# One product for G and b, pairs of full products early in TensorE's queue, and a new order of the first 911 steps

## The chip, the core and the metric

The kernel runs on one core of one Trainium2 chip. The core has five engines with queues of their own, each strictly in its program's order: TensorE (PE, with its weight loads PEld), VectorE (DVE), ScalarE (ACT), GpSimd (POOL) and SyncE (SP), which here issues all DMAs. The metric is the device time of one execution in microseconds; lower is better.

## The reference

Three parts follow one another: a gated linear attention with a running maximum, and two hidden layers.

```python
for t in range(S):                                # B=4, H=8, S=768, D=40
    m_new = maximum(f[t] + m, i[t])
    C = exp(f[t] + m - m_new) * C + exp(i[t] - m_new) * outer(v[t], k[t])
    n = exp(f[t] + m - m_new) * n + exp(i[t] - m_new) * k[t]
    y[t] = sigmoid(o[t]) * (C @ q[t]) / maximum(abs(n @ q[t]), 1)
x = y as (3072, 320)
h = x @ w_in;  x = (h * clip(h + 3, 0, 6) / 6) @ w_out       # 320 -> 2048 -> 320
h = x @ w_in2; out = square(maximum(h, 0)) @ w_out2          # 320 -> 2048 -> 320
```

## The kernel before

**Attention** goes by units: one batch b and one chunk c of 64 positions, all 8 heads; 48 units, in the order (b, c) = (0,0) (1,0) (0,1) (1,1) (2,0) (3,0) (2,1) (3,1), then by chunk. gate_m, gate_g, gate_G and gate_b are scans and sums over the gates on VectorE, once for chunks 0 to 3 and once for the rest. They give G, a running sum of log forget gates, and b, the log input gate less the maximum and G. A unit's weights are exp(G[query] + b[key] + causal mask). For units 0 to 15, w_pe makes the exponent on TensorE in PSUM (Wp) and w_e takes exp on ScalarE. For units 16 and on, at_gload, w_add and w_mask make it from a DMA and GpSimd. at_S is q times k (Sp, fp32, 16 small products), at_P multiplies it by the weights (VectorE), x_k scales keys, at_Y makes the output and the new state (Yp, 32 small products of 41 columns), at_C copies the state on for the batch's next unit, and at_n1, at_n2, at_n3 divide by max(|n q|, 1) and multiply by the output gate's sigmoid (o_load, o_sig), into X.

**w_pe before**: a product of the mask; then the row b and, per head, G. Rows 0 to 63 of the tile pre hold for each batch a table R of which row belongs to which head (head_rows), and gb holds b as high and low part. For chunks 0 and 1 a unit has eight products of 64 columns that pick G's row (sel, L383) and one of 512 columns for b (L386). For chunks 2 and 3 G is read back through a DMA (at_G, at_R) into four more rows of pre, so one product of 68 rows does it.

**Hidden layers** go by slots: mm_A (L650, hps), one group of 128 hidden units for 512 columns (for slots 0 to 15: 256), eight products; act1, act1b, act2, act2b on ScalarE and VectorE; mm_B (L691, acc), for each 128 tokens three products of 320 columns. Slot s is (layer, block of tokens, group). t_pe, t_hi, t_lo transpose X into high and low parts (xs) for mm_A. Weights arrive as 64-bit floats and are made into high and low parts by w_load (DMA), w_exp (ScalarE), w_b1, w_b2 (VectorE), w_hi (ScalarE) and w_lo (GpSimd, or VectorE with @v); w_load:0,i is group i//2, in-weights for even i.

**Order.** Everything is issued in one list: first FIRST, a list of steps written out (name:unit or name:slot,part; a suffix @v, @a or @g puts the step on VectorE, ScalarE or GpSimd), then the rest in an order that the function moe makes. Each engine takes its own instructions from that list in order and waits where data or buffers are not ready. FIRST reaches to about slot 39 of 200. Buffers that matter: qkt has 3, kI 3, Z 2 for each batch, Sp, tp and Wp of units 8 and on share one PSUM buffer ("s"). Gp (G as high and low part) shares its buffer with the last out-weights, w_load:0,15, and pre shares one of two with xs.

**warm** before: warm:4 issues four fp32 products of 512 columns at the start, on the identity.

Of the kernel before, what the change touches and what calls it, by code (L numbers as in the profile page):

```python
# [37 lines left out]
at_n2:0 at_S:2 x_k:2 w_e:3 at_P:1,0 w_exp:0,2 w_pe:4 w_lo:0,0@v at_load:5 w_pe:5 w_b1:0,2 w_e:4  # L38
at_n3:0 w_load:0,4 w_exp:0,1 at_Y:1 at_P:2,0 w_load:0,10 w_e:5 w_b1:0,1 at_Y:2 at_C:1 at_n1:1
at_S:3 x_k:3 at_n1:2 at_C:2 at_n2:2 w_pe:6 w_load:0,6 at_n2:1 at_n3:2@g at_P:3,0 w_e:6 at_n3:1  # L40
at_Y:3 w_b2:0,2 t_pe:0,0,0 at_C:3 w_pe:7 at_n1:3 t_hi:0,0,0 at_load:6 w_hi:0,2 at_n2:3 at_n3:3
w_e:7 t_lo:0,0,0 w_lo:0,2 w_exp:0,4 t_pe:0,0,1 t_hi:0,0,1 t_lo:0,0,1 w_b1:0,4 at_R mm_A:0
w_exp:0,10 w_load:0,5 w_b2:0,4 mm_A:1 act1:0 w_b2:0,1 w_hi:0,4 at_S:4 act1b:0 x_k:4 act1:1
at_load:7 act2:0 act1b:1 w_lo:0,4 w_hi:0,1 act2b:0 at_P:4,0 mm_A:2 w_exp:0,6 load_gates:1 act2:1
at_S:5 w_lo:0,1 act1:2 act2b:1 w_load:0,3 act1b:2 at_Y:4 at_P:5,0 act2:2 x_k:5 mm_A:3 at_C:4
act2b:2 at_load:8 w_b1:0,6 w_exp:0,5 mm_A:4 w_b2:0,6 act1:3 at_S:6 act1:4 w_load:0,8 w_b1:0,5
w_hi:0,6 mm_B:0,0 w_b2:0,5 mm_B:0,1 mm_B:1,1 act1b:3 x_k:6 w_hi:0,5 mm_B:1,0 at_P:6,0 act2:3
w_lo:0,5 act2b:3 at_load:9 w_pe:8 w_exp:0,3 at_n1:4 mm_A:5 at_n2:4 w_e:8 w_lo:0,6 w_load:0,7
act1b:4 at_Y:5 act1:5 act2:4 act1b:5 w_pe:9 at_C:5 act2b:4 w_e:9 at_n3:4@g at_n1:5 mm_A:6 at_n2:5
o_load:1 at_S:7 w_b1:0,3 act1:6 w_b2:0,3 w_exp:0,8 at_Y:6 act1b:6 x_k:7 w_hi:0,3 at_P:7,0  # L50
w_load:0,14 at_C:6 w_lo:0,3 at_n1:6 at_S:8 x_k:8@a at_n2:6 at_Y:7 at_P:8,0 at_n3:6@g mm_B:2,1
at_n1:7 mm_B:3,1 at_n3:5 w_exp:0,7 t_pe:0,0,2 w_load:0,9 mm_B:4,1 at_n2:7 at_C:7 mm_B:2,0
t_hi:0,0,2@v at_n3:7@g mm_B:3,0 act2:5 t_lo:0,0,2 at_Y:8 act2:6 act2b:5 o_sig:1 t_pe:0,0,3 act2b:6
mm_B:4,0 w_load:0,12 w_b1:0,7 mm_B:5,1 mm_B:5,0 w_b2:0,7 mm_A:7 w_b1:0,8 t_hi:0,0,3 w_b2:0,8 act1:7
w_hi:0,7 at_load:10 t_lo:0,0,3 at_C:8 w_lo:0,7 act1b:7 w_hi:0,8 mm_A:8 at_n1:8 w_load:0,13 act2:7
at_S:9 act1:8 x_k:9@v w_exp:0,9 act1b:8 w_lo:0,8 mm_B:6,0 at_P:9,0 mm_B:6,1 act2:8 at_n2:8@a
act2b:8 w_pe:10 at_load:11 act2b:7 mm_B:8,3 gate_m:1 mm_A:9 at_load:12 mm_A:10 w_exp:0,12 gate_g:1
w_load:0,11 mm_B:7,1 act1:9 mm_B:7,0 act1:10 act1b:9 gate_G:1 at_Y:9 w_e:10 mm_B:8,2 act1b:10
act2:9 at_S:10 x_k:10 act2b:9 w_exp:0,13 at_load:13 w_b1:0,10 mm_A:11 act2:10 at_C:9 act2b:10
mm_B:9,3 w_exp:0,14 w_b2:0,10 mm_A:12 o_load:2 act1:11 at_P:10,0 w_hi:0,10 mm_B:10,3 act1b:11  # L60
w_pe:11 w_load:0,15 act1:12 at_n3:8 mm_B:9,2 act2:11 act1b:12 w_lo:0,10 mm_B:10,2 w_e:11 act2b:11
act2:12 at_n1:9 mm_A:13 w_exp:0,11 act2b:12 w_b1:0,9 o_load:3 mm_A:14 act1:13 w_b1:0,12 mm_B:11,3
act1b:13 act1:14 at_S:11 x_k:11 at_n2:9 act2:13 act1b:14 o_sig:2 mm_B:11,2 act2b:13 at_load:14
mm_B:12,2 w_b2:0,9 mm_A:15 w_b2:0,12 mm_B:13,2 mm_B:12,3 act1:15 at_P:11,0 mm_B:13,3 act2:14
act1b:15 w_pe:12 w_hi:0,12 act2b:14 at_Y:10 gate_b:1 act2:15 w_e:12 mm_A:16 gate_bT:1 o_load:5
act2b:15 at_C:10 mm_B:14,2 o_load:4 at_n1:10 act1:16 at_S:12 x_k:12 w_lo:0,12@v w_hi:0,9 mm_B:15,2
mm_B:14,3 at_n2:10@a at_P:12,0 w_lo:0,9 mm_B:15,3 at_load:15 act1b:16 w_pe:13 mm_A:17 w_b1:0,11
w_e:13 w_b2:0,11 act2:16 at_n3:9 at_Y:11 w_hi:0,11 act2b:16 at_n3:10@g w_pe:14 act1:17 at_n1:11
mm_B:16,0 w_e:14 w_lo:0,11 mm_B:16,2 act1b:17 at_C:11 mm_B:16,1 at_n2:11 act2:17 at_S:13 o_sig:3
act2b:17 x_k:13 mm_A:18 at_P:13,0 at_n3:11@g at_load:16 w_b1:0,13 mm_B:17,2 act1:18 mm_A:19  # L70
w_b2:0,13 w_exp:0,15 act1b:18 w_hi:0,13 w_b1:0,15 mm_B:17,0 act2:18 w_b2:0,15 at_Y:12 act1:19
act2b:18 w_lo:0,13 w_pe:15 at_gload:16 at_gload:17 at_C:12 mm_B:16,3 at_n1:12 w_e:15 mm_A:20
act1b:19 w_add:17 at_n2:12@a w_b1:0,14 at_S:14 w_b2:0,14 mm_B:17,3 mm_B:18,3 at_P:14,0 w_mask:17
# [810 lines left out]
```

## Time and profile before

| | us |
|---|---|
| median of 3 runs (lowest, highest) | 844.32 (844.25, 846.9) |
| the profiled execution | 845.29 |
| its span, first to last instruction | 843.4 |
| TensorE busy, share of the span | 829.6, 98% |
| VectorE, ScalarE, GpSimd busy | 524.8, 433.4, 205.6 |
| mean granted TensorE clock | 0.972 |

The granted clock is the share of 2.4 GHz that TensorE was given; 0.50 is 1.2 GHz. Busy TensorE time includes products at either clock. A wait names the instruction that ended it.

### The profile page before, as it was taken

Reading aid. Unit: us, or ns where it says so; the run is one execution under the profiler, and the core shown is the slowest. Engines: PE = TensorE matmul, PEld = TensorE weight load, DVE = VectorE, ACT = ScalarE, POOL = GpSimd, SP = SyncE. Lnnn points to the kernel's source line nnn. Section 1 sums busy time; section 2 is a strip of 40 time slices with the busy share of each in tenths; the row PEclk is TensorE's granted clock in tenths of the full one; section 3 lists DMA queues with packets and bytes.
Section 4 is the critical chain, followed back from the end, with each engine's and each line's share of the span. In section 5 each row is a group of like instructions: output and inputs, shape, how many; then the busy total and the mean of one; then the engine's idle time right before and its main releaser. Section 6 shows DMA issues by size and latency. Waiting matters only on the chain.

```text
span 843.4 us, 19370 instructions
## 1 busy us (share of the span) xinstructions
PE 829.6 (98%) x8040; PEld 735.3 (87%) x8040; DVE 524.8 (62%) x947; ACT 433.4 (51%) x805; POOL 205.6 (24%) x191
## 2 busy tenths in 40 slices
...
GB/s 220 179 216 186 184 69 96 114 110 88 78 93 108 102 91 118 86 108 21 2 52 194 205 99 1 1 33 1 30 3 1 32 1 2 32 1 1 31 1 32
DMA packets 28843, 63.67 MB, mean 75 GB/s; under 512 B 4912, under 2 KB 17264, under 8 KB 28752
## 3 DMA queue, kind: packets, MB, share of 16 engines
...
q14 instruction: 24, 0.20, 0.1%
HBM read 58.39 MB, written 4.03 MB: 74 GB/s over the span
## 4 chain that ended last, share of the span: by engine, by line
PE 94%; ACT 2%; issue 2%; DVE 2%; POOL 1%; ACTq 0%; POOLq 0%; DVEq 0%
PE hps L650 41%; PE acc L691 39%; PE Yp L504 4%; PE tp L626 2%; PE Sp L470 2%; PE Sp L462 1%; PE Wp L383 1%; PE Sp L464 1%; PE Wp L386 1%; PE Wp L376 1%; PE Sp L477 0%; ACT qs L446 0%; ACT X L698 0%; ACT g L659 0%; DVE qs L448 0%
## 5 line engine op out<-in xcount | busy, mean ns | idle before, releaser
L650 PE MATMUL hps<-xs,wi 128*128 128x512 f32 (+1 forms) x1600 | 390.4, 387 | 1.2 <-ACT xs L630 1.1
L691 PE MATMUL acc<-wo,gh 128*128 128x320 f32 x1536 | 350.0, 315 | 0.2 <-POOL wo L611 0.2
L650 PEld LDWEIGHTS hps<-xs,wi 128*128 128x128 f32 x1600 | 288.2, 191 | 50.9 <-ACT xs L630 1.5
L691 PEld LDWEIGHTS acc<-wo,gh 128*128 128x128 f32 x1536 | 259.8, 189 | 10.5 <-POOL wo L611 0.4
L691 PE MATMUL acc<-wo,gl 128*128 128x320 f32 x768 | 238.0, 310 | 0.0
L681 DVE TENSOR_TENSOR gl<-g,gh 128x512 fp32r<-128x512 f32 x176 | 127.5, 726 | 65.5 <-ACT gh L676 64.7
L671 DVE TENSOR_TENSOR g<-g 128x512 f32<-128x512 f32 x96 | 66.4, 692 | 127.6 <-ACT g L661 127.1
L691 PEld LDWEIGHTS acc<-wo,gl 128*128 128x128 f32 x768 | 144.9, 189 | 0.0
L676 ACT CAST gh<-g 128x512 fp32r<-128x512 f32 x172 | 106.5, 619 | 66.8 <-DVE g L671 53.4
L659 ACT ACTIVATE g<-hps,three 128x512 f32<-128x512 f32 (+1 forms) x104 | 68.1, 656 | 132.0 <-PE hps L650 128.7
L661 ACT ACTIVATE g<-hps 128x512 f32<-128x512 f32 x96 | 57.4, 598 | 151.4 <-PE hps L650 149.5
L668 DVE SCALAR_TENSOR_TENSOR g<-g,hps 128x512 f32<-128x512 f32 x80 | 54.7, 684 | 52.9 <-ACT g L659 52.8
L426 POOL TENSOR_TENSOR Xm<-qkt,W 40x512 f32<-40x512 f32 x27 | 35.8, 1324 | 92.4 <-ACT W L416 74.6
L611 POOL TENSOR_TENSOR wi<-wt,wi 128x768 fp32r<-128x768 f32 x13 | 24.9, 1916 | 108.5 <-ACT wi L606 100.0
L504 PEld LDWEIGHTS Yp<-Z,Xm 104*32 104x32 f32 (+1 forms) x3072 | 35.7, 111 | 16.5 <-issue 14.4
L393 POOL TENSOR_TENSOR W<-W,bT 104x512 f32<-104x512 f32 x32 | 43.5, 1358 | 20.5 <-DVE rd L517 9.0
L448 DVE SCALAR_TENSOR_TENSOR qs<-qs,less,qkt 120x512 fp32r<-120x512 f32 x52 | 40.2, 813 | 9.7 <-ACT qs L446 9.4
L504 PE MATMUL Yp<-Z,Xm 104*32 104x41 f32 (+1 forms) x3072 | 41.8, 210 | 2.8 <-issue 2.8
L437 POOL TENSOR_TENSOR Xm<-kI,W 104x320 f32<-104x320 f32 x37 | 33.7, 911 | 36.5 <-ACT W L406 21.6
L611 POOL TENSOR_TENSOR wo<-wt,wo 128x640 fp32r<-128x640 f32 x16 | 26.6, 1661 | 37.0 <-ACT wo L606 28.1
L446 ACT CAST qs<-qkt 120x1024 fp32r<-120x1024 f32 x26 | 27.2, 1048 | 7.2 <-PE acc L691 3.5
L543 DVE TENSOR_TENSOR X<-X,yt 64x320 f32<-64x320 f32 x34 | 25.3, 743 | 0.9
(110 smaller groups left out, 688.8 us busy)
## 6 DMA issues: line engine op xcount, KB each, us to landing
...
```

The costliest lines, as they stand in the source:

```text
L393: on("w_add", "g", u).tensor_tensor(out=W, in0=W, in1=bT[:, c - NC1, b * H:(b + 1) * H].unsqueeze(2).to_broadcast([KX, H, L]), op=ALU.add)
L448: nc.vector.scalar_tensor_tensor(out=y[0:KS, i], in0=y[0:KS, i].bitcast(F32), scalar=less[0:KS, i:i + 1], in1=x[0:KS, i], op0=ALU.mult, op ...
L504: nc.tensor.matmul(out=Yp[o:e, h, :], lhsT=Xm[:, h, o:e], rhs=Z[b][c % 2][:, h, :], start=True, stop=True)
L611: on("w_lo", "g", ph, i).tensor_tensor(out=w[:, 1], in0=f, in1=w[:, 0].bitcast(F32), op=ALU.subtract)
L650: nc.tensor.matmul(out=h, lhsT=w[:, hl, kk, o:o + P], rhs=t[:, xk, i0 * P:i1 * P], start=(i == 0), stop=(i == len(TERMS) - 1))
L659: nc.scalar.activation(out=g, in_=T["h", s], func=ACTF.Relu, bias=three)
L661: nc.scalar.activation(out=g, in_=T["h", s], func=ACTF.Relu)
L668: nc.vector.scalar_tensor_tensor(out=g, in0=r, scalar=6.0, in1=T["h", s], op0=ALU.min, op1=ALU.mult)
L671: nc.vector.tensor_tensor(out=g, in0=r, in1=r, op=ALU.mult)
L676: copy("act2", s)(out=gh, in_=g)
L681: nc.vector.tensor_tensor(out=gl, in0=g, in1=gh.bitcast(F32), op=ALU.subtract)
L691: nc.tensor.matmul(out=acc[i], lhsT=g[:, n], rhs=w[:, hl, m % MG, :], start=(m == 0 and q == 0), stop=(m == NM - 1 and q == 2))
```

## The change

Chunks 0 to 3 now take one product of 128 rows. A new step, at_rg, writes into rows 64 to 127 of pre the table R times G of the unit's chunk; gb has ones there, so the product sums b and G. The eight products per head, sel, const_s, at_G, at_R and the DRAM buffer Gd1 go. at_load becomes at_qk, at_kn and at_va. at_n1 takes the reciprocal first, clears its sign bit, and the minimum with 1 moves into at_n2 (or stays in at_n1 where ScalarE does at_n2). warm:i issues two bf16 products of 128 rows and 512 columns; 13 such steps stand in the first part of FIRST. FIRST is new.

```diff
 FIRST = """
-const_z:1 const_i warm:4 load_gates:0 const_o head_rows:3 at_load:0 const_m const_l const_g const_z:3
-head_rows:1 o_load:0 const_z:0 const_z:2 at_load:1 const_k:1 const_k:0 gate_m:0 w_load:0,0 gate_g:0
-at_S:0 gate_G:0 const_s at_G:0 gate_b:0 at_load:2 o_sig:0 gate_bT:0@v head_rows:0@v w_load:0,2
-at_S:1 const_k:2 w_pe:0 head_rows:2@g w_pe:1 w_e:0 at_G:1 w_load:0,1 w_exp:0,0 w_pe:2 at_P:0,0
-x_k:0 w_e:1 w_b1:0,0 at_Y:0 at_load:3 w_e:2 w_b2:0,0 w_pe:3 at_C:0 at_n1:0 x_k:1 w_hi:0,0 at_load:4
...
+const_g load_gates:0 const_z:0 const_z:2 const_i const_z:3 warm:1 const_m const_l head_rows:1
+const_z:1 const_o warm:8 at_kn:0 head_rows:3 at_kn:1 const_k:2 warm:13 const_k:0 at_qk:0 const_k:1
+head_rows:2 at_qk:1 warm:16 gate_m:0 at_qk:2 at_va:0 warm:18 gate_g:0 head_rows:0 at_va:1 at_S:0
+gate_G:0 at_va:2 at_qk:3 gate_b:0 at_S:1 at_rg:0@v gate_bT:0 at_kn:2 at_va:3 w_load:0,0 w_pe:0
+at_rg:1@v o_load:0 w_load:0,1 w_pe:1 w_e:0 at_rg:2 w_load:0,4 warm:22 warm:23 w_e:1 at_qk:4 x_k:0@v
+at_P:1,0 w_pe:2 at_rg:3 w_exp:0,0 warm:25 at_P:0,0 x_k:1 w_e:2 warm:33 at_Y:0 at_kn:3 w_b1:0,0
+w_load:0,2 at_Y:1 w_b2:0,0 o_sig:0 w_load:0,7 w_pe:3 at_S:2 at_rg:4@v at_n1:0 x_k:2 w_pe:4 at_n2:0
+at_S:3 at_rg:5 at_C:0@v at_qk:5 w_exp:0,1 at_n1:1 warm:35 at_n2:1 w_hi:0,0 at_n3:0@g warm:36
+at_P:2,0 warm:37 w_e:3 at_va:4 w_lo:0,0@v at_Y:2 at_va:5 warm:38 at_n3:1 at_va:6 w_exp:0,4 at_P:3,0
+w_pe:5 at_va:7 x_k:3@v at_va:8 at_S:4 at_C:1 at_rg:6@v at_C:2 w_e:4 at_Y:3 at_va:9 at_n1:2
+w_exp:0,2 at_n2:2 w_pe:6 at_rg:7 at_n1:3 at_n3:2@g w_e:5 at_n2:3 w_e:6 w_pe:7 at_P:4,0 at_kn:4
+at_rg:8 w_exp:0,7 at_kn:5 t_pe:0,0,0 w_e:7 w_load:0,5 at_n3:3 at_C:3 w_load:0,3 w_b1:0,2 t_hi:0,0,0
+at_qk:6 w_b2:0,2 at_qk:7 at_kn:6 t_lo:0,0,0 w_hi:0,2 x_k:4 at_kn:7 t_pe:0,0,1 w_b1:0,1 at_Y:4
+t_hi:0,0,1 w_b2:0,1 at_va:10 t_lo:0,0,1 w_lo:0,2 w_hi:0,1 at_n1:4 w_exp:0,5 mm_A:0 w_load:0,10
...
+act1b:9 act2:8 at_S:8 act2b:8 x_k:8@a act2:9@v mm_A:10 w_b1:0,9 gate_G:1 mm_B:8,3 o_sig:2 mm_B:8,2
...
+at_n2:13 at_S:14 at_n3:13 w_exp:0,15 x_k:14 mm_B:17,3 act1:21 at_P:14,0 at_gload:18 mm_B:18,3
...
-    NC0 = 2
-    KW = 2 * BH + 2 * (NC1 - NC0)
     pre = xs_p.tile([P, 5, TB], F32R, tag="xs", name="pre")
-    R = [pre[0:KW, b] for b in range(B)]
-    gb = pre[0:KW, B, 0:NC1 * KX].rearrange("p (c k) -> p c k", k=KX)
-    sel = pre[0:2 * BH, B, NC1 * KX:NC1 * KX + BH]
+    R = [pre[0:2 * BH, b] for b in range(B)]
+    RG = [pre[2 * BH:P, b] for b in range(B)]
+    gb = pre[:, B, 0:NC1 * KX].rearrange("p (c k) -> p c k", k=KX)
...
         nc.vector.memset(gb[0:2 * BH].bitcast(F32), 0.0)
-
-        k = slice(2 * BH, KW)
-        shape = [KW - 2 * BH, NC1 - NC0, KX]
-        nc.vector.memset(gb[k, 0:NC0].bitcast(F32), 0.0)
-        nc.vector.tensor_tensor(
-            out=gb[k, NC0:], in0=ident[k, 2 * BH:KW:2].unsqueeze(2).to_broadcast(shape),
-            in1=ident[k, 2 * BH + 1:KW:2].unsqueeze(2).to_broadcast(shape), op=ALU.add)
+        nc.vector.memset(gb[2 * BH:P].bitcast(F32), 1.0)
...
+    def at_rg(u):
+        b, c = units[u]
+        on("at_rg", "g", u).tensor_tensor(
+            out=RG[b].rearrange("p (h l) -> p h l", l=L),
+            in0=R[b].rearrange("p (h l) -> p h l", l=L).bitcast(F32),
+            in1=Gp[:, c * L:(c + 1) * L].unsqueeze(1).to_broadcast([2 * BH, H, L]).bitcast(F32),
+            op=ALU.mult)
...
-        k = KW
-        if c < NC0:
-            k = 2 * BH
-            for h in range(H):
-                j = b * H + h
-                nc.tensor.matmul(
-                    out=Wp[:, h * L:(h + 1) * L], lhsT=sel[:, j:j + 1].to_broadcast([k, KX]),
-                    rhs=Gp[:, c * L:(c + 1) * L], start=False, stop=False)
-        nc.tensor.matmul(out=Wp, lhsT=gb[0:k, c], rhs=R[b][0:k], start=False, stop=True)
+        nc.tensor.matmul(out=Wp, lhsT=gb[:, c], rhs=pre[:, b], start=False, stop=True)
...
+        nc.vector.reciprocal(out=rd, in_=Yp[0:L, :, D:DV])
+        bits = rd.bitcast(I32)
         nc.vector.tensor_scalar(
-            out=rd, in0=Yp[0:L, :, D:DV], scalar1=-1.0, scalar2=1.0, op0=ALU.mult, op1=ALU.max)
-        nc.vector.tensor_tensor(out=rd, in0=Yp[0:L, :, D:DV], in1=rd, op=ALU.max)
-        nc.vector.reciprocal(out=rd, in_=rd)
+            out=bits, in0=bits, scalar1=2 ** 31 - 1, scalar2=None, op0=ALU.bitwise_and)
+        if ENG.get(("at_n2", u)) == "a":
+            nc.vector.tensor_scalar(out=rd, in0=rd, scalar1=1.0, scalar2=None, op0=ALU.min)
...
-            nc.vector.tensor_tensor(
-                out=yt[p0:p0 + L], in0=Yp[0:L, :, 0:D], in1=rd.to_broadcast([L, H, D]),
-                op=ALU.mult)
+            nc.vector.scalar_tensor_tensor(
+                out=yt[p0:p0 + L], in0=rd.to_broadcast([L, H, D]), scalar=1.0,
+                in1=Yp[0:L, :, 0:D], op0=ALU.min, op1=ALU.mult)
...
-    def warm(n):
+    def warm(i):
+        one = ident.bitcast(BF16)
         t = ps_acc.tile([P, TB], F32, tag="acc1", name="warm")
-        for _ in range(n):
+        for _ in range(2):
             nc.tensor.matmul(
-                out=t, lhsT=ident, rhs=ident.unsqueeze(1).to_broadcast([P, TB // P, P]),
+                out=t, lhsT=one[:, 0:P], rhs=one.unsqueeze(1).to_broadcast([P, TB // (2 * P), 2 * P]),
                 start=True, stop=True)
```

## Rows read from the trace of the kernel before

**Rows 1.** Windows by stage: length, busy PE, PEld, DVE, ACT, POOL, clock, DMA share, GB/s.
```profile
0.00:11.40 11.40, 8.67 (x81) 5.02 (x81) 9.51 (x28) 7.54 (x9) 4.26 (x18) 1.00 0.71 205
11.40:39.60 28.20, 27.15 (x397) 22.22 (x397) 13.18 (x33) 12.28 (x22) 6.89 (x7) 0.51 0.64 215
39.60:52.40 12.80, 12.79 (x160) 11.84 (x161) 8.48 (x16) 6.46 (x12) 4.81 (x4) 0.50 0.34 108
52.40:67.20 14.80, 12.02 (x283) 10.21 (x284) 9.11 (x26) 9.65 (x22) 6.62 (x6) 0.96 0.91 323
67.20:73.20 6.00, 6.00 (x89) 5.54 (x83) 3.42 (x10) 2.04 (x6) 1.53 (x2) 0.50 0.82 210
73.20:90.00 16.80, 15.78 (x274) 14.02 (x274) 14.58 (x28) 15.42 (x32) 4.96 (x5) 1.00 0.28 82
90.00:200.00 110.00, 110.00 (x1651) 94.15 (x1650) 90.72 (x186) 79.05 (x194) 52.52 (x49) 1.00 0.44 121
200.00:385.00 185.00, 182.38 (x2316) 161.03 (x2314) 143.59 (x268) 103.64 (x173) 88.39 (x79) 1.00 0.35 93
```

**Rows 2.** Windows of 0.5 us where the granted clock turns, same columns.
```profile
11.50:12.00 0.50, 0.50 (x3) 0.39 (x3) 0.22 (x1) 0.16 (x2) 0.00 (x0) 0.72 0.80 173
...
52.50:53.00 0.50, 0.50 (x5) 0.50 (x5) 0.47 (x2) 0.21 (x1) 0.00 (x0) 0.82 0.83 174
```

**Rows 3.** The chain that ended last, in order of time: start, length, what.
```profile
10.94 0.43 DVE pre L277
...
12.35 1.26 PE Wp L383 x8
...
13.62 0.55 PE Wp L386
...
14.16 0.43 PE Wp L376
...
20.06 0.26 PE Sp L462
...
21.95 0.59 PE Wp L376
...
39.20 0.36 ACT xs L630
...
39.61 4.03 PE hps L650 x16
...
49.44 1.24 PE Yp L504 x61
...
50.68 3.00 PE hps L650 x16
```

**Rows 4.** Groups by shape, 11.4 to 39.6 us: busy, mean ns, idle before.
```profile
L383 PE MATMUL Wp<-Gp,pre 64*104 64x64 f32 x56 | 12.8, 389 | 0.0
...
L486 DVE TENSOR_TENSOR Xm<-Sp,W 104x512 f32<-104x512 f32 x4 | 2.7, 683 | 0.9 <-ACT W L406 0.9
...
L597 DVE SCALAR_TENSOR_TENSOR wt<-rwi,wt 128x768 int32<-128x768 int32 x2 | 1.9, 952 | 0.0
```

**Rows 5.** Waits, 11.4 to 39.6 us: total, times, longest.
```profile
DVE rd L517 <- ACT Z L512: 6.8, 3, 2.6
```

**Rows 6.** Single lines over the span: ns min/median/max, first and last start.
```profile
L519 DVE TENSOR_TENSOR rd<-Yp,rd x48: 156/157/158, 18.4 to 413.3; 64x8 f32<-64x8 f32 x48
...
L437 POOL TENSOR_TENSOR Xm<-kI,W x37: 727/872/1376, 12.7 to 396.6; 104x320 f32<-104x320 f32 x37
...
L437 DVE TENSOR_TENSOR Xm<-kI,W x4: 473/480/1046, 78.9 to 172.0; 104x320 f32<-104x320 f32 x4
...
L426 POOL TENSOR_TENSOR Xm<-qkt,W x27: 1285/1293/1616, 132.7 to 395.2; 40x512 f32<-40x512 f32 x27
...
L426 DVE TENSOR_TENSOR Xm<-qkt,W x5: 689/725/1710, 132.4 to 211.2; 40x512 f32<-40x512 f32 x5
...
L611 POOL TENSOR_TENSOR wi<-wt,wi x13: 1811/1846/2099, 36.7 to 532.5; 128x768 fp32r<-128x768 f32 x13
```

172 lines of the change are left out of this document (79 added, 93 removed).

## The prediction

> **What bounds the kernel now.** I read the stages first [rows 1]. From 90 us on TensorE is busy without a gap (110.00 of 110 us, then 182.38 of 185) at the full granted clock, 1.00, with VectorE below it (90.72 of 110). Nothing but less TensorE work could shorten that part, and there the change removes none and only reorders. Everything else must come from the first 90 us, and two losses stand there. The clock is at 0.51 and 0.50 (1.2 GHz) from 11.4 to 52.4 us and again from 67.2 to 73.2. And TensorE has gaps: about 1 us in the second stage, 2.8 in 52.4 to 67.2, 1.0 in 73.2 to 90, the page's busy time being the generous reading of them.
>
> Next, where the clock turns [rows 2]. The mean of 0.72 says that it fell inside 11.5 to 12.0, the 0.82 that it rose inside 52.5 to 53.0. Then what stood there, in the chain that ended last [rows 3]: before the fall, one gate chain on VectorE that ends in a head row (10.94, 0.43) and small products of attention. Before the rise, 1.24 us of Yp and 3.00 us of hps, back to back. An earlier 4.03 us of hps at 39.61 did not raise it: ahead of it TensorE had waited for ScalarE (the 39.20 row is the last piece), behind it came the small Sp products.
>
> Last, that TensorE is the chain between 11.4 and 37.8, so its half rate costs there, and how full the others are: VectorE 13.18 of 28.20 us, ScalarE 12.28 [rows 1]. VectorE's longest idle in that stretch, 6.8 us ahead of L517, hangs on ScalarE's copy of Yp [rows 5], which itself waits for TensorE.
>
> **The change, part by part.** *The products of w_pe.* Eight units lose eight products of 64 columns each. These 64 are the costliest group of the stretch (56 of them after 11.4: 12.8 us busy, 389 ns each, overlapped) [rows 4]. On the chain eight take 1.26 at half rate [rows 3], so 8 x 1.26 = 10.1 us leave TensorE. What stays of a unit is 0.43 (the mask) and 0.55 (the one product, now of 128 rows instead of 64) [rows 3]. More rows of the same 512 columns I price at nothing: the columns stream one after another in either. If that were wrong the product could at most double, 8 x 0.55 = 4.4 us at half rate, or gain nothing.
>
> *at_rg.* Sixteen new multiplications of 64 x 512, four on VectorE (units 0, 1, 4, 6), twelve on GpSimd. No row has this shape. Nearest is x_q, 40 x 512: 0.69 to 1.71 on VectorE, 1.29 to 1.62 on GpSimd [rows 6]. I take 0.69 and 1.29 and keep 1.71 and 1.62 for the range. GpSimd holds 6.89 us of work in 28.20 [rows 1], so 12 x 1.29 = 15.5 us spread over some 110 us lie beside other work, but each is now a wait of TensorE's queue: w_pe stands in order ahead of hidden-layer products. RG has one buffer for each batch, so at_rg waits for the w_pe of the batch's previous unit, which is long past. If that cover fails see the third rival.
>
> *VectorE before the first product.* Two head rows (0.43 each [rows 3]), const_s, a small memset and the row sums in const_o go; a memset and at_rg:0 (0.69) come. I estimate 1 us less, so the first product closes at 10.4 instead of 11.4; without it every time below is 1 us later.
>
> *at_n1 and at_n2.* One instruction of 0.157 less for each unit (reciprocal and a mask of the sign bit in place of three), or the same number where ScalarE does at_n2. 48 of them are at most 7.5 us of VectorE; beside a TensorE that is full from 90 on they are worth nothing, before that some 16 x 0.157 = 2.5 us.
>
> *The pairs.* Five stand before Sp of unit 0 and only replace the old warm-up. Eight stand between the first w_pe and Yp of unit 2 or 3: sixteen products of 512 columns. The nearest row is the mask product, 0.43 at half rate [rows 3], so 6.9 us at half and 3.4 at full. From the first w_pe on TensorE's order is three units of 0.98 and four pairs: 2.9 + 3.4 = 6.3 us with nothing small in it before Yp. That is longer than the 4.24 us of Yp and hps in whose course it rose before [rows 3], so I take the clock to be up by about 16 us instead of 52.7.
>
> *DMA order.* at_load is split in three. On SP's queue the first weight load now stands behind at_qk:3, which needs the tile that Sp of unit 0 gives back; behind it wait kn, va and then the weights, so they are issued some 4 us later. ScalarE's w_exp:0,0, w_e:2 behind it and VectorE's w_b1:0,0 are late by part of that; I put it in the waits below. The last weight load, 0,15, now waits for at_rg:15, since Gp shares its buffer. Between that step and mm_B:22, which needs it, the order holds three full mm_A and over a dozen mm_B: its conversion is covered by them.
>
> *Stage 1, up to mm_A:0 (before: 39.6).* With TensorE at full rate VectorE is the next limit. Its 13.2 us [rows 1] get three at_rg (2.1), two key scalings at 0.48 [rows 6], one at_P of 0.68, one w_b2 of 0.95 [rows 4], and a t_lo pair and a state copy, both taken like at_P; less four times 0.157 [rows 6] and one at_n3. About 18 us in all. From 10.4 that ends at 28.4. Waits that it cannot fill (the first W, the weights, the last transpose and its copies) I estimate at 4 us of the 15.0 that it idled here before. So mm_A:0 stands at 32.5: **7.1 us earlier**. Bounds: without waits 10.5. At half rate throughout, TensorE's own 28.2 lose 10.1, gain 6.9 of pairs, Sp of unit 4 (20.06 to 21.95, 1.9) and Yp of unit 4 (1.24): 28.1, so mm_A:0 at 38.5 and 1.1 us.
>
> *Stage 2, mm_A:0 to where before stands at 90.* It took 50.4 us. TensorE's work at full rate is 12.79/2 + 11.5 + 6.00/2 + 15.78 = 36.7 [rows 1]. VectorE's is 8.48 + 9.11 + 3.42 + 14.58 = 35.6, less some 3 that moved ahead of mm_A:0 or went; at its share of the last of these stages (14.58 of 16.80, 0.87) that is 37.5. Two engines that both want 37 do not fit perfectly: I take 40, **10.4 us saved**. Bounds: 36 (14.4 saved), and 46.4 (4.0 saved) if the clock comes up only as late after mm_A:0 as before (6.4 us lost).
>
> From 90 on: 0, between -2.6 (all the idle of 200 to 385) and +3. Sum: 843.4 - 7.1 - 10.4 = 825.9 of span. The profiled execution took 845.29, 1.9 more than its span, and the median of the runs is 844.32, 1.0 below it: **827 us**, 2.1% faster. About 0.3%, 2.5 us, is what tells a change from none here.
>
> **Rivals.** *The clock does not hold.* Yp and Sp again stand behind the pairs, and such products stood before the fall at 11.7. Then 1.1 + 4.0 = 5 us: 839. For it: the 4.03 us that raised nothing; against: the dense stretch is longer and without a gap.
>
> *VectorE pays for GpSimd.* x_k on VectorE takes 0.47 to 1.05 and x_q 0.69 to 1.71 [rows 6]: something beside them stretches them by up to 1.02. Twelve more GpSimd instructions could each stretch one of VectorE's: 12 x 1.02 = 12.2, and VectorE is the limit I count on: 839. If all sit on the path and stage 1's 4 us of waits double, 843, no change. The Trainium skill, "SBUF — State Buffer", Who interferes with whom, goes further: a VectorE instruction with two SBUF inputs and a GpSimd one that reads SBUF shut each other out for the whole length. At 1.29 that would be 15.5 us, 842. The trace shows doubled VectorE rows, but none that says what doubled them.
>
> *Slower: w_pe waits for at_rg.* For units 8 to 15 at_rg stands on GpSimd between w_lo (1.85) and x_k (0.87) [rows 6], some only one Yp ahead of their w_pe. A wait of 1.85 + 1.29 = 3.1 us for each of eight units is 25 us, 827 + 25 = 852. It decides from 17.5/8 = 2.2 us a unit. Against: w_pe 8 and on need the Sp buffer and so leave GpSimd time.
>
> *More than forecast.* Both best bounds and the idle of 200 to 385: 10.5 + 14.4 + 2.6 = 27.5, so 817.
>
> **How the numbers follow.** Forecast 0.52 (its own range 819 to 834), clock 0.20, VectorE behind GpSimd 0.10 (half of it no change), slower 0.10, more 0.08. Faster: 0.52 + 0.20 + 0.05 + 0.08 = 0.85; same 0.05; slower 0.10. The range from 814 to 842 holds all but the slow case and the far ends of the others.
>
> **What would show it.** The granted clock is 1.00 from about 16 to 40 us and does not fall near 67. L383 is gone and L386 has 16 products no longer than 0.55 at half rate. The first hps starts near 32. VectorE's share from 11 to 32 is above 0.8. The step that stands before at 90 comes near 72. It is wrong if TensorE waits for at_rg (an idle Wp released by GpSimd), if the first hps starts after 37, or if stages past 90 show more than 5 us of idle.

## The result, and the profile after

The changed kernel takes **853.4 us** (median of 4 runs, 851.27 to 856.55) beside 844.3 of before, run together with it: ratio 1.0124 with a 95% interval of 1.0089 to 1.0158 (the ratio, here and below, is not the quotient of the two medians, which is 1.0108). It is 1.2% slower; 827 us was forecast, within 814 to 842. The profiled execution took 853.42 us, its span 851.6.

The stages of after, by the same boundaries and columns as [rows 1]:

```profile
0.00:11.40 11.40, 8.98 (x79) 3.80 (x80) 9.15 (x25) 7.39 (x12) 3.83 (x17) 0.95 0.51 121
11.40:39.60 28.20, 21.58 (x384) 11.21 (x383) 15.87 (x31) 14.41 (x21) 9.71 (x10) 0.72 0.73 255
39.60:52.40 12.80, 10.66 (x130) 9.77 (x131) 11.45 (x20) 7.07 (x13) 5.22 (x3) 0.56 0.59 217
52.40:67.20 14.80, 14.44 (x257) 12.36 (x256) 10.74 (x23) 9.18 (x18) 7.63 (x6) 0.92 0.32 88
67.20:73.20 6.00, 3.64 (x81) 3.06 (x81) 5.73 (x11) 5.40 (x9) 3.43 (x3) 1.00 0.97 342
73.20:90.00 16.80, 15.41 (x262) 13.90 (x262) 15.81 (x29) 13.61 (x28) 7.25 (x7) 0.90 0.68 231
90.00:200.00 110.00, 105.22 (x1581) 88.52 (x1570) 87.68 (x160) 59.29 (x143) 52.30 (x49) 0.98 0.34 92
200.00:385.00 185.00, 182.20 (x2307) 160.17 (x2305) 148.04 (x253) 107.41 (x192) 91.50 (x83) 1.00 0.39 98
```

Read TensorE's column first. Over the whole span it is busy 825.4 us instead of 829.6, so there is less work in it, as forecast. But it idles 851.6 - 825.4 = 26.2 us instead of 13.8. Of these 12.4 us more, 7.7 lie ahead of 90 us (the first six rows sum to 74.71 busy, those of before to 82.41) and 4.8 between 90 and 200, where before had none. What ended the idle, 9 to 160 us (engine and line, what it waited for, total, times, longest):

```profile
PE Sp L448 <- issue: 3.6, 1, 3.6
PE Yp L490 <- DVE Xm L479: 3.4, 1, 3.4
PE tp L615 <- ACT wo L595: 3.1, 1, 3.1
PE tp L615 <- DVE xs L626: 2.6, 1, 2.6
PE hps L639 <- DVE xs L624: 1.5, 1, 1.5
```

Five single pauses make 14.2 us, and they have four causes: only the last two are of one kind, transposed pieces of X (xs) that VectorE brings late. Before had none above 2.1 us there. The clock follows them. Windows between its turns, same columns as above:

```profile
10.50:17.10 6.60, 6.49 (x40) 1.98 (x43) 4.26 (x7) 3.95 (x6) 3.39 (x3) 0.50 1.00 358
17.30:20.50 3.20, 2.07 (x111) 1.40 (x98) 2.63 (x8) 3.18 (x4) 2.50 (x3) 1.00 1.05 333
20.70:30.80 10.10, 7.73 (x67) 4.31 (x67) 3.72 (x6) 1.93 (x4) 0.16 (x1) 0.50 0.56 184
30.90:41.00 10.10, 7.05 (x239) 4.62 (x238) 6.71 (x14) 6.28 (x11) 5.30 (x5) 1.00 0.55 188
41.20:54.60 13.40, 11.51 (x131) 10.58 (x131) 10.92 (x20) 6.68 (x12) 4.08 (x3) 0.50 0.56 207
```

It rises at 17.2 us, where the prediction put it (16), but falls in the course of the first pause. It is up again from 30.85 and falls after the 2.6 us pause. The first hps starts at 41.0, not at 32.5, and before had it at 39.6 [rows 3].

How the lead went, by the start of act1 in each slot: slot 0 stands at 47.0 (before 42.0), slot 12 at 88.6 (90.5), slot 24 at 153.2 (150.7), slot 27 at 168.5 (159.4). From slot 40 on the loss stays at 8.3 to 8.4 us to the end. These marks move with the order, so a lead in them is not yet a lead in work. Count work as TensorE's busy time times the granted clock. From 39.6 to 90 us the four rows of after give 36.8 us of it, those of before 36.7 [rows 1]: nothing was won back there. Between 90 and 200, after pauses for 4.8 us and loses 1.7 more to a stretch at half rate (157.1 to 160.6), 6.5 us in all, where before lost nothing; behind 200 both idle alike (6.1 to 6.2 us). Of the 8.2 us between the spans, then, 1.7 were lost by 90 us and 6.5 behind it.

Single lines over the span of after (ns min/median/max, first and last start; L372 takes the place of L386, and L506 that of L517 and of L519 in [rows 6]):

```profile
L348 POOL TENSOR_TENSOR pre<-pre,Gp x12: 1264/1281/1754, 10.4 to 114.5; 64x512 fp32r<-64x512 f32 x12
L348 DVE TENSOR_TENSOR pre<-pre,Gp x4: 684/685/685, 8.7 to 29.1; 64x512 fp32r<-64x512 f32 x4
...
L372 PE MATMUL Wp<-pre x16: 474/478/753, 9.9 to 120.2; 128*104 128x512 f32 x16
...
L698 PE MATMUL warm<-ident x26: 379/631/650, 1.8 to 31.8; 128*128 128x512 bf16 x26
...
L506 DVE TENSOR_SCALAR rd<-rd x48: 162/165/1412, 18.0 to 421.7; 64x8 int32<-64x8 int32 x48
```

And of before:

```profile
L386 PE MATMUL Wp<-pre x16: 475/497/731, 11.4 to 118.1; 64*104 64x512 f32 x8, 68*104 68x512 f32 x8
L517 DVE TENSOR_SCALAR rd<-Yp x48: 146/150/159, 18.2 to 413.1; 64x8 f32<-64x8 f32 x48
```

### The profile page after: what moved, and what is told of

Read it like the earlier page. It is cut to its first block, busy times and chain, and to the rows that moved or that the text cites. A ratio compares the mean times of both kernels' runs of the same rounds, so it can differ in the third digit from the quotient of the medians.

```text
span 851.6 us, 19211 instructions
## 1 busy us (share of the span) xinstructions
PE 825.4 (97%) x7994; PEld 721.6 (85%) x7994; DVE 544.8 (64%) x911; ACT 425.1 (50%) x780; POOL 220.7 (26%) x200
## 3 DMA queue, kind: packets, MB, share of 16 engines
q1 hardware_dynamic: 28588, 62.38, 24.4%
## 4 chain that ended last, share of the span: by engine, by line
PE 83%; DVE 8%; ACT 3%; issue 3%; DMA 2%; POOL 1%; SPq 1%; POOLq 0%; ACTq 0%; DVEq 0%
PE hps L639 37%; PE acc L680 36%; PE Yp L490 3%; PE tp L615 2%; PE Sp L456 2%; DVE qs L434 1%; DVE wt L586 1%; DMA qkt<-in_qk 1%; ACT yt L519 1%; PE warm L698 1%; PE Sp L448 1%; DVE rd L506 1%; DMA rwo<-in_w1o 1%; PE Sp L450 1%; DVE gl L670 1%
## 5 line engine op out<-in xcount | busy, mean ns | idle before, releaser
L680 PEld LDWEIGHTS acc<-wo,gh 128*128 128x128 f32 x1536 | 258.8, 188 | 10.4 <-ACT gh L665 0.3
L657 DVE SCALAR_TENSOR_TENSOR g<-g,hps 128x512 f32<-128x512 f32 x80 | 54.7, 684 | 47.5 <-ACT g L648 47.3
L412 POOL TENSOR_TENSOR Xm<-qkt,W 40x512 f32<-40x512 f32 x31 | 41.2, 1329 | 116.8 <-ACT W L402 81.2
L600 POOL TENSOR_TENSOR wi<-wt,wi 128x768 fp32r<-128x768 f32 x15 | 28.4, 1892 | 114.6 <-ACT wi L595 114.6
L490 PEld LDWEIGHTS Yp<-Z,Xm 104*32 104x32 f32 (+1 forms) x3072 | 33.8, 107 | 18.1 <-issue 11.1
L379 POOL TENSOR_TENSOR W<-W,bT 104x512 f32<-104x512 f32 x32 | 43.4, 1357 | 11.1 <-DMA W<-Gd 10.7
L490 PE MATMUL Yp<-Z,Xm 104*32 104x41 f32 (+1 forms) x3072 | 39.7, 205 | 4.2 <-DVE Xm L479 3.4
L532 DVE TENSOR_TENSOR X<-X,yt 64x320 f32<-64x320 f32 x38 | 31.9, 838 | 6.3 <-ACT yt L519 5.3
L423 POOL TENSOR_TENSOR Xm<-kI,W 104x320 f32<-104x320 f32 x35 | 31.1, 889 | 7.0 <-PE Yp L490 4.9
L615 PE MATMUL tp<-ident,X 128*128 128x128 f32 x144 | 23.6, 273 | 6.3 <-ACT wo L595 3.1
```

What stands on the lines that cost most here:

```text
L379: on("w_add", "g", u).tensor_tensor(out=W, in0=W, in1=bT[:, c - NC1, b * H:(b + 1) * H].unsqueeze(2).to_broadcast([KX, H, L]), op=ALU.add)
L490: nc.tensor.matmul(out=Yp[o:e, h, :], lhsT=Xm[:, h, o:e], rhs=Z[b][c % 2][:, h, :], start=True, stop=True)
L600: on("w_lo", "g", ph, i).tensor_tensor(out=w[:, 1], in0=f, in1=w[:, 0].bitcast(F32), op=ALU.subtract)
L657: nc.vector.scalar_tensor_tensor(out=g, in0=r, scalar=6.0, in1=T["h", s], op0=ALU.min, op1=ALU.mult)
L680: nc.tensor.matmul(out=acc[i], lhsT=g[:, n], rhs=w[:, hl, m % MG, :], start=(m == 0 and q == 0), stop=(m == NM - 1 and q == 2))
```

## The experiments

"Before" is its median in runs beside those of each kernel. It moved between 841.1 and 844.6 from one set to the next, and a ratio is uncertain by 0.2 to 0.5%, so two kernels of different sets are told apart from about 0.5% on. The ratio and the quotient of the medians differ by up to 0.3 points (e16: 837.4 / 842.9 is 0.9935). Idle is the profiled span less TensorE's busy time, from one profile of each. Kernels that start from before (e1, e5, e9, e10, e12, e15, e16) keep its first warm-up, warm:4; the others have the new one, the five early pairs.

| run | what it is | us | before | ratio (95%) | span | idle |
|---|---|---|---|---|---|---|
| e1 | old order, product of 128 rows | 845.7 | 841.1 | 1.0035 (1.0004 to 1.0066) | 844.9 | 21.0 |
| e2 | after, no pairs | 845.8 | 841.1 | 1.0055 (1.0022 to 1.0089) | 842.8 | 23.4 |
| e3 | after, three loads later | 848.5 | 841.1 | 1.0085 (1.0049 to 1.0120) | 844.8 | 22.6 |
| e4 | after, three places mended | 854.3 | 841.1 | 1.0145 (1.0094 to 1.0196) | 849.6 | 24.4 |
| e5 | e1, at_rg behind x_k | 838.6 | 844.6 | **0.9935** (0.9904 to 0.9967) | 836.0 | 18.2 |
| e6 | e2, engines of units 16, 17, 19 | 844.0 | 844.6 | 0.9998 (0.9974 to 1.0023) | 841.7 | 22.3 |
| e7 | e17, five loads later | 850.6 | 844.6 | 1.0074 (1.0035 to 1.0113) | 848.9 | 24.7 |
| e8 | e7, no pairs | 848.1 | 844.6 | 1.0048 (1.0025 to 1.0071) | 846.1 | 26.9 |
| e9 | e5 with the pairs | 842.0 | 842.3 | 1.0010 (0.9990 to 1.0029) | 841.9 | 19.0 |
| e10 | e5, three loads later | 839.0 | 842.3 | 0.9951 (0.9924 to 0.9978) | 833.7 | 14.0 |
| e11 | e6, ScalarE's order at 63 us | 847.7 | 842.3 | 1.0059 (1.0040 to 1.0078) | 844.0 | 20.6 |
| e12 | e5 with the new at_n1, at_n2 | 843.4 | 842.3 | 1.0012 (0.9987 to 1.0037) | 841.5 | 20.9 |
| e13 | after with the old at_n1, at_n2 | 850.1 | 842.9 | 1.0084 (1.0052 to 1.0116) | 854.2 | 20.8 |
| e14 | e6 with the old at_n1, at_n2 | 843.7 | 842.9 | 0.9992 (0.9964 to 1.0019) | 840.8 | 18.3 |
| e15 | e5, head_rows:2 first on GpSimd | 838.6 | 842.9 | 0.9936 (0.9906 to 0.9965) | 836.5 | 17.4 |
| e16 | e15 and e10 | 837.4 | 842.9 | **0.9901** (0.9864 to 0.9938) | 838.0 | 14.5 |
| e17 | after, engines of units 16, 17, 19 | 849.5 | 842.1 | 1.0082 (1.0042 to 1.0121) | 848.3 | 23.0 |

**The product alone.** e1 and e5 put the product of 128 rows into the kernel before, order, warm-up and at_n1 unchanged:

```diff
- ... gate_G:0 const_s at_G:0 gate_b:0 ... head_rows:0@v ... w_pe:0 head_rows:2@g w_pe:1 ... w_pe:2 at_P:0,0 x_k:0
+ ... gate_G:0 gate_b:0 ... head_rows:0@v at_rg:0@v at_rg:1@v ... w_pe:0 at_rg:2 head_rows:2@g at_rg:4 at_rg:5 w_pe:1 at_rg:3 ... x_k:0   (e1)
+ ... w_pe:0 at_rg:2 head_rows:2@g w_pe:1 ... w_pe:2 at_P:0,0 x_k:0 at_rg:3 at_rg:4 ... x_k:1 at_rg:5   (e5)
```

> The order of the kernel before, with only the product of 128 rows in it (G and b in one tile, at_rg on VectorE for units 0 and 1 and on GpSimd for the rest, no pairs). If the new order is what loses, this is faster than before: the eight products of 1.26 us at half rate (10 us) are gone and the waits of the old order stay, so 835 to 841 us. If the product of 128 rows itself or at_rg beside VectorE loses, it is at or above before, 844 to 852 us.

> As e1_old_order, but at_rg:3, at_rg:4 and at_rg:5 stand behind x_k:0 and x_k:1 on GpSimd, where e1 had a pause of 5.70 us on TensorE at 14 us (Yp waits for Xm behind three at_rg of 1.58 us). If the product of 128 rows is a gain that e1 only lost in this place, the first act1 comes 4 to 5 us ahead of before instead of 0.8, and the time is 836 to 842 us; where the lead is lost again at a later instruction fetch (73 us in e1), 841 to 845 us. If at_rg beside VectorE costs as much as the products saved, it stays at 844 to 847 us.

e1 fell outside its first theory, because of one place: TensorE stood 5.7 us for GpSimd's x_k behind three at_rg. With that mended the product is a gain, 0.65%, and the first act1 stands at 36.4, 5.6 us ahead of before. TensorE's busy time falls from 829.6 to 817.8, by 11.8 us, of which 4.4 come back as idle time (18.2 beside 13.8).

**The pairs**, taken out of after (e2) and put into e5 (e9):

```diff
- ... w_load:0,4 warm:22 warm:23 w_e:1 ... w_exp:0,0 warm:25 at_P:0,0 x_k:1 w_e:2 warm:33 at_Y:0 ...   (e2, and 35 to 38)
+ ... w_pe:1 warm:22 warm:23 at_rg:3 ... w_exp:0,0 warm:25 ... w_e:2 warm:33 ... at_P:3,0 warm:38   (e9)
```

> The changed kernel without the eight pairs (warm:22 to warm:38). If the pairs hold the clock up from 17 to 20 us and from 31 to 41 us, as the prediction had it, the first 40 us pass at half rate and the time is 856 to 860 us. If they only fill pauses that are there anyway, it stays within 0.3% of the changed kernel, 851 to 856 us; if they stand in the way of later work on the tensor engine, 846 to 850 us.

> e5_old_order_rg with the eight pairs of the changed kernel put behind the same steps (w_pe:1 twice, w_exp:0,0, w_e:2, at_n1:1, at_n2:1, at_Y:2, at_P:3,0). The prediction's theory: the pairs stand in pauses and keep the clock up, so the time is at or below e5, 834 to 839 us. The other theory: TensorE has hardly a pause there (2.1 us of them before 30 us in e5), so the sixteen products of 0.24 us at full and 0.5 us at half rate lie on its path, and the time is 4 to 8 us above e5, 842 to 847 us.

Both speak for their last theory, pairs that lie on TensorE's path: 1.0124 against 1.0055 and 1.0010 against 0.9935, 0.7% or some 6 us for eight pairs. e2 stays even a little below what that theory gave it (845.8 beside 846 to 850). In e9 the clock does stay up on them, from 6.5 to 20.2 us where e5 falls at 13.9. It then falls in the course of this wait for at_rg on GpSimd, 18 to 23 us of e9:

```profile
PE Wp L363 <- POOL pre L339: 2.6, 1, 2.6
```

By the page the sixteen products add 822.9 - 817.8 = 5.1 us to TensorE's busy time, at whatever clock they won.

**TensorE's own instructions.** The chain around the longest pause of after shows a wait for nothing, in the middle of one unit's Sp:

```profile
19.29 0.07 PE Sp L448 x2
19.37 3.59 issue
22.96 0.33 PE Sp L448
```

e3 and e7 move loads away from it (e7 has the engines of e17 as well):

```diff
- ... w_load:0,4 warm:22 ... w_load:0,2 at_Y:1 ... w_load:0,7 ... at_qk:5 w_exp:0,1 ...
+ ... at_qk:5 w_load:0,4 w_load:0,2 w_load:0,7 w_exp:0,1 ...   (e3)
+ ... at_qk:5 w_load:0,1 w_load:0,2 o_load:0 w_load:0,4 w_load:0,7 ... w_exp:0,1 o_sig:0 w_exp:0,4 ...   (e7)
```

> The changed kernel with the weight loads 4, 2 and 7 of the first pass issued behind the load at_qk:5, so that fewer bytes are under way at 19 to 23 us. Theory: TensorE's pause of 3.59 us at 19.37 is its own instruction fetch (a packet on the instruction queue at 20.43) that waits behind these loads. Then the pause shrinks below 1 us, the clock does not fall at 20.6, and the time is 844 to 850 us. Rival: the pause is something else in TensorE's instruction stream; it stays at about 3.6 us and the time at 851 to 855 us.

> The changed kernel (pairs kept) with o_load:0 and the weight loads 1, 2, 4 and 7 all behind at_qk:5, and with the mended engines of e6. Theory (TensorE's instruction packet is asked for when 193 of its instructions are through, waits behind the queued loads, and TensorE goes on 1.4 us after it lands): the packet starts within 1 us of that point, at about 14.5 us, the pause at instruction 449 is gone, and the clock does not fall at 18 to 21 us; 840 to 847 us. Rival: the pause at instruction 449 stays 1.5 us or more with the DMA engines free, so its length is fixed by something else.

> As e7 without the pairs. If the pairs are on TensorE's path all the same, it is 5 to 8 us below e7; if without the instruction pause they do hold the clock at full and pay for themselves, it is within 2 us of e7 or above it. Beside before: 834 to 842 us by the first, 842 to 848 us by the second.

In e7 and e8 the sigmoid of the first og tile comes behind the first at_n3 products, so that part of their output is not the reference's; the work is the same.

Now count instructions up to the end of the pause, in after, e2, e3 and e4 (one window each, from 0):

```profile
0.00:22.90 22.90, 16.83 (x223) 7.07 (x223) 15.92 (x37) 16.39 (x23) 9.18 (x22) 0.80 0.76 248
```
```profile
0.00:19.60 19.60, 13.40 (x223) 7.35 (x223) 15.79 (x34) 13.83 (x20) 9.03 (x22) 0.81 0.74 237
```
```profile
0.00:18.75 18.75, 13.36 (x223) 6.38 (x223) 14.84 (x31) 12.88 (x19) 8.94 (x21) 1.00 0.64 195
```
```profile
0.00:21.50 21.50, 16.98 (x223) 7.41 (x223) 15.93 (x37) 14.97 (x21) 9.21 (x22) 0.83 0.73 232
```

In e3 the pause is 2.3 us instead of 3.6, not below 1 as its theory had it, and the clock falls at 18.6; its 848.5 us lie in the theory's range, but its interval overlaps that of after. Of the four windows: four kernels, four times, one count: 223 products and 223 weight loads, which with three semaphore and drain instructions in the record makes 449. In e2 eight products came out ahead of it, and still it is the 223rd. So the pause belongs to the place in the instruction stream. Before's pause of 2.1 us at 62.75 ends at 1729 and e5's of 2.5 us at 64.0 at 1985: 449 + 5 x 256 and 449 + 6 x 256. The DMA view names what comes just before the end: in 19.4 to 20.4 us of after only data packets, in 20.4 to 20.5 one packet of instructions (queue, kind, packets, MB, share):

```profile
q1 hardware_dynamic: 85, 0.26, 105.3%
...
q8 instruction: 1, 0.02, 75.7%
```

That packet holds 16,384 bytes. It starts at 20.43, takes 1.21, and TensorE goes on 1.32 us after it lands. In e2, e3, e4, e13 and at before's pause that last step is 1.27 to 1.51 us, in e5 1.47 and 1.61. When does the packet start? Around 256 instructions ahead: in e7, with the DMA engines idle, TensorE reached its instruction 193 at 17.06 and the packet started at 17.67. In after it was reached at 16.7 and the packet started at 20.43, when the queued loads ran out (DMA share 1.05 up to 20.5). In e7 TensorE runs through instruction 449 (at 20.49) without a break:

```profile
16.40:18.00 1.60, 1.60 (x62) 1.01 (x64) 1.38 (x2) 0.81 (x1) 0.00 (x0) 0.50 0.04 10
18.00:20.40 2.40, 2.40 (x87) 1.62 (x78) 1.89 (x5) 0.02 (x1) 1.84 (x2) 0.59 0.00 0
```

So the theory holds as to the pause. As to the time it bought nothing: e7 took 850.6 us (840 to 847 by its theory) beside 849.5 of e17, from which it differs by those moves alone, and e8, 1.0048, is 0.5% slower than e6, 0.9998, although e6's pause of 1.7 us is gone in it. In e7 VectorE's at_n3 now waits 8.3 us for o_load:0, and Sp behind it 4.0 us at 28.6; the clock falls at 23.4 all the same. Between e7 and e8 the pairs cost 0.26% or 2.5 us, which fits neither of e8's cases and is not clear of noise. The theory's second test was in the old order:

```diff
- ... at_P:7,0 w_load:0,14 ... w_load:0,12 w_b1:0,7 ... at_load:10 ... w_load:0,13 act2:7 ... at_load:11 ...
+ ... at_load:10 w_load:0,12 ... at_load:11 w_load:0,13 w_load:0,14 ...   (e10)
```

> e5_old_order_rg with the weight loads 12, 13 and 14 of the first pass moved behind at_load:10 and at_load:11, which frees the DMA engines from about 58 us on. Theory (the pauses of 1.36 us at 57.1 and 2.55 us at 64.0 are instruction packets behind these loads): the packets start within 1.5 us of instructions 1473 and 1729, both pauses go, the clock does not fall at 58.3, and 4 to 6 us are saved: 832 to 836 us. Rival: the pauses stay or the later loads hold up w_exp:0,12 or w_exp:0,14, and the time stays at 837 to 841 us.

Waits of e5, then of e10, 9 to 100 us:

```profile
PE Yp L480 <- issue: 4.4, 3, 2.5
```
```profile
PE Yp L480 <- issue: 1.1, 2, 0.7
```

The pause of 2.5 us went and the one of 1.4 halved, and the span is 2.3 us shorter, but the clock fell at 58.6 all the same, and the timed runs do not tell e10 from e5: the rival's range.

**Places in the new order.**

```diff
- ... w_b1:0,2 t_hi:0,0,0 at_qk:6 w_b2:0,2 ... t_lo:0,0,0 ...
+ ... t_hi:0,0,0 at_qk:6 ... t_lo:0,0,0 w_b1:0,2 w_b2:0,2 ...   (e4; likewise w_b1, w_b2 of 0,1 and 0,7)
- ... o_sig:1 mm_B:4,0 ... t_hi:0,0,3 ...
+ ... mm_B:4,0 ... t_hi:0,0,3 o_sig:1 ...   (e4, e11; e11 also t_hi:0,0,2@v at_n3:7@g)
- at_n3:16 ... at_n3:17 ... x_k:19@v
+ at_n3:16@g ... at_n3:17@g ... x_k:19@a   (e4, e6, e7, e8, e11, e14, e17)
```

> The changed kernel with three places of the order mended: t_lo:0,0,0 and t_lo:0,0,1 ahead of the weights' steps on VectorE (pauses of 2.65 and 1.51 us at 37.2 and 41.6); o_sig:1 behind t_hi:0,0,3 and t_lo:0,0,2 ahead of w_b1 and w_b2 of 0,7 (3.05 us at 70.8); at_n3:16, at_n3:17 on GpSimd and x_k:19 on ScalarE as before had them (3.39 us at 153.8). If these waits are what is lost, the pauses go and the clock holds past 75 and 157: 10.6 us of pauses and up to 2 us of clock back, 841 to 846 us. If each pause only comes back behind the next late work, 850 to 854 us.

> e6_no_pairs_n3 with o_sig:1 behind t_hi:0,0,3, with t_hi:0,0,2 on VectorE and at_n3:7 on GpSimd as before had them, and with w_b1 and w_b2 of 0,7 behind t_lo:0,0,2. If the pause of 3.03 us at 63.5 (tp waits for ScalarE) and the fall of the clock at 66.7 that follows it are this place of the order alone, 4 to 6 us come back against e6: 836 to 840 us, below before. If VectorE and ScalarE are simply behind with their whole queue there, the pause moves and 842 to 846 us stay.

> The changed kernel without the eight pairs and with at_n3:16, at_n3:17 on GpSimd and x_k:19 on ScalarE. In e2 the lead over before fell from 6 us (slot 25) to 0 (slot 27); if the VectorE queue ahead of Xm of unit 18 is what loses it, 3 to 4 us stay, and the time is 837 to 843 us, at or below before. If another wait takes its place, 843 to 847 us as e2.

> The changed kernel with at_n3:16, at_n3:17 on GpSimd and x_k:19 on ScalarE, nothing else. If that place costs in the changed kernel what it cost without the pairs (e6 against e2: 0.57%, 4.8 us), the pause of 3.39 us at 153.8 and the half clock of 3.5 us behind it go, and the time is 1.005 to 1.008 of before, 847 to 850 us. If TensorE waits for the next late work instead, it stays at 1.010 to 1.014, 852 to 855 us.

The first two places did not mend. In e4 the wait for ScalarE's wo (3.1 us) goes, those for VectorE's xs are 3.8 us instead of 4.1, and waits of hps for gl (4.1 us) and for ScalarE's xs (2.6 us) come in, and the time is 854.3; in e11 3.0 us become 1.5 and 2.2, and 847.7 us are above both of its ranges. That VectorE and ScalarE are late there with their whole queue fits this but is not shown. The third place did go: the pause of 3.4 us at 153.8 is gone in e17 (0.7 us of another wait stand there), its span is 3.3 us shorter, and the time 849.5, as expected. The intervals of e17 and after overlap; those of e6 and e2, the same edit without the pairs, hardly touch (0.9998 against 1.0055), though e6's 844.0 us is not the gain that its first theory wanted.

**The new at_n1**, put into e5 (e12) and taken from after (e13) and e6 (e14):

```diff
-        nc.vector.tensor_scalar(out=rd, in0=Yp[0:L, :, D:DV], scalar1=-1.0, scalar2=1.0, op0=ALU.mult, op1=ALU.max)
-        nc.vector.tensor_tensor(out=rd, in0=Yp[0:L, :, D:DV], in1=rd, op=ALU.max)
-        nc.vector.reciprocal(out=rd, in_=rd)
+        nc.vector.reciprocal(out=rd, in_=Yp[0:L, :, D:DV])
+        nc.vector.tensor_scalar(out=bits, in0=bits, scalar1=2 ** 31 - 1, scalar2=None, op0=ALU.bitwise_and)
```

> e5_old_order_rg with at_n1 and at_n2 of the changed kernel (reciprocal first, then the sign bit masked off in SBUF, the minimum with 1 folded into the product). If the mask in SBUF, which took 0.16 to 1.41 us beside GpSimd, costs time, 840 to 844 us; if one VectorE operation fewer per unit is a gain, 835 to 838 us; if neither is on the path, within 0.3% of e5, 836 to 841 us.

> The changed kernel with at_n1 and at_n2 of the kernel before. If the sign mask in SBUF, whose 48 instructions took 502 ns each in e12 against 153 and 158 ns for the two on PSUM, costs as much here as it did in the old order (e12 against e5: 0.8%), the time is 846 to 849 us. If VectorE's queue has room for it in this order, it stays at 851 to 856 us.

> e6_no_pairs_n3 with at_n1 and at_n2 of the kernel before: only the product of 128 rows and the new order are left of the change. If the new order itself is what loses, it is at or above before in spite of the saved products, 842 to 846 us (e6 had 1.000 of before). If the mask is what e6 still lost against e5, it comes to 836 to 840 us, as e5.

In e5's order it costs 0.8%. In the new order it is not shown to cost anything: e13 and after overlap (850.1 us, between its two ranges), e14 and e6 agree. e14's 843.7 us fit its first case, in which the order itself loses. That the stretched mask is what costs e12 its time is likely, but no run parts it from the change to at_n2. What stretches it is plain in the timelines of GpSimd and of VectorE in after (start, length):

```profile
40.06 1.84 POOL L600 TENSOR_TENSOR wi<-wt,wi 128x768 fp32r<-128x768 f32 x1 [2.41 <-ACT wi L595]
43.42 1.55 POOL L600 TENSOR_TENSOR wo<-wt,wo 128x640 fp32r<-128x640 f32 x1 [1.52 <-ACT wo L595]
```
```profile
40.26 2.32 DVE L586 SCALAR_TENSOR_TENSOR wt<-rwo,wt 128x640 int32<-128x640 int32 x1
42.61 0.42 DVE L624 TENSOR_TENSOR xs<-tp,xs 128x256 fp32r<-128x256 f32 x1
43.07 0.29 DVE L626 TENSOR_TENSOR xs<-tp,xs 64x128 fp32r<-64x128 f32 x1
43.39 0.20 DVE L504 RECIPROCAL rd<-Yp 64x8 f32<-64x8 f32 x1
43.63 1.37 DVE L506 TENSOR_SCALAR rd<-rd 64x8 int32<-64x8 int32 x1
```

GpSimd's second row ends at 44.97, and the mask of 64x8 that starts in its course ends at 45.00: 1.37 us for what takes 0.165 alone. The w_b2 above it starts 0.2 us behind GpSimd's first row and ends 0.7 us behind it. Over the whole of after, 17 of the 48 masks take more than 0.2 us, and each of the 17 ends 0.02 to 0.03 us behind a GpSimd instruction that had started before it; the other 31 take at most 0.165. L504, which reads PSUM, lies across the start of GpSimd's row and keeps its 0.20 us, as L519 kept its 0.157 in all 48 units of [rows 6].

**The rest of the old order.**

```diff
- ... w_pe:0 at_rg:2 head_rows:2@g w_pe:1 ...
+ ... head_rows:2@g w_pe:0 at_rg:2 w_pe:1 ...   (e15; e16: with the loads of e10)
```

> e5_old_order_rg with head_rows:2 ahead of the first at_rg on GpSimd, which idles there. The pause of 0.97 us at 13.9 us (Yp waits for GpSimd's Xm) should shrink by about 1 us: 836 to 839 us. If TensorE then only comes earlier to a packet of instructions that is not there, as at 57 and 64 us in e5, nothing is gained and it stays within 0.3% of e5.

> e10_loads_later with the same move of head_rows:2. Both moves together: 831 to 837 us if the later loads help, as the profile of e10 has it (its span is 2.3 us below that of e5); 837 to 840 us if e10 gained nothing over e5, as its timed runs have it (0.995 of before against 0.9935).

The pause at 13.9 us is gone in e15 and the time unchanged, the second of its cases. e16 has the lowest median and ratio of all, 837.4 us and 0.9901, but its interval overlaps those of e5, e10 and e15, from which it is not told apart. All four beat both kernels.

## Why the prediction was wrong

The span was to be 825.9 and is 851.6. Of the 25.7 us between them 19.2 belong to the first 90 us, where 17.5 were to be saved and 1.7 were lost, and 6.5 to what follows.

*Products of w_pe, at_rg: right.* The eight products are gone, at_rg takes 0.684 on VectorE and 1.264 to 1.754 on GpSimd against 0.69 and 1.29 forecast, the 128 rows cost next to nothing (474 ns at least and 753 at most, 475 and 731 before), and the first product closes at 9.85 instead of 10.4 us. Alone they make the kernel 0.65% faster (e5): 11.8 us less of TensorE's work where 10.1 were priced, and 4.4 us of new waits.

*Pairs and clock: the step that failed first.* The price at half rate, 6.9 us, was near: warm's busy time, overlaps taken out, grew from 5.4 to 12.9 us, of which the eight pairs are 7.8, seven of them at half rate. That they would pay by the clock ("I take the clock to be up by about 16 us") failed. It rose at 17.2 and fell 3.4 us later, in the first pause; the sum had taken for granted that nothing would stop TensorE from then on. So stage 1's path was wrong as well ("With TensorE at full rate VectorE is the next limit"): in the first three windows between the clock's turns VectorE is busy 10.6 of 19.9 us, 0.53 where above 0.8 was to be seen, and TensorE 16.3, most of it at half rate. In either order the pairs cost about 6 us.

*DMA order and stage 1's "waits that it cannot fill", estimated at 4 us: mis-sized, and with a cause that the prediction did not have.* It saw that the weight loads come late and at once, and counted only their lateness. They also fill the DMA engines just when TensorE wants its next instructions. The first hps came 8.5 us later than forecast, with 4 us of waits already in the forecast. Towards these 12.5 us, 3.6 are this pause, 2.65 the second transpose, which stands behind w_b1 and w_b2 of 0,2 on VectorE, and 3.9 the half clock from 20.6 to 30.8 us (7.73 us of busy time at half); the other 2.4 are not assigned. What the pause is worth in time stays open, since e7 and e8 took it away and gained nothing. (A slip of the sum that decides nothing: without its 4 us of waits stage 1 saves 11.1 us, not 10.5.)

*Stage 2: nothing of its 10.4 us.* At slot 12 the kernel is 1.9 us ahead of before although it started slots 5 us late, but that is the order of the slots: from 39.6 to 90 us TensorE did the work of before, 36.8 us of it, which the sum wanted done in 40. The clock was to be up and was at half rate from 41.1 to 54.7 and 75.2 to 78.6. *"From 90 on: 0" failed*, with a bound, +3, that the loss left by far: 4.8 us of pauses and 2% of clock over 110 us. The largest pause stands where the new order gives VectorE two at_n3 and x_k:19 ahead of unit 18's Xm; x_k:19 took 1.95 us beside GpSimd.

*at_n1: wrong in sign where a run could tell.* One instruction less was priced at a gain of up to 2.5 us. e12 measured a loss of 0.8%, for at_n1 and at_n2 together.

*The rivals.* "VectorE pays for GpSimd" (0.10) happens, though it was priced for at_rg alone, and it is the mask, w_b2 and x_k that pay. In the rows at 40.26 and 43.63 VectorE started second and ended with GpSimd or behind it. The Trainium skill, "SBUF — State Buffer", Who interferes with whom, says that a VectorE instruction with two SBUF inputs contends with a GpSimd one that reads SBUF, and that one in a 2-port mode, which tensor_scalar can enter, is blocked for the whole of a GpSimd instruction that issued first. The trace agrees for w_b2 (two SBUF inputs, 2.32 us instead of 0.81 at least); that the mask, a tensor_scalar, ran in such a mode no run here shows. "w_pe waits for at_rg" is not what made after slower, and that its 852 lies near the 853.4 measured is chance. It is there in small in e9 and e12 (2.6 and 1.7 us). "The clock does not hold" (0.20) came true, but together with the pauses, which its 839 did not have.

*The account.* From before to after by one chain of kernels: product alone -0.65% (e5); the new order with its split loads and new warm-up +0.57% (e14); the new at_n1 and at_n2 +0.06% (e6); engines of units 16, 17 and 19 +0.57% (e2); pairs +0.69% (after). These add up to the measured 1.24% because each is the difference of two neighbours, so the sum proves nothing; each step is uncertain by 0.3 to 0.5%. Taken elsewhere the parts are not the same: the engines cost 0.4% with the pairs in (e17), at_n1 0.8% and the pairs 0.75% in the old order. Of the order's 0.57% the cause stays open, and the new warm-up was never run by itself. The profiles of e14 and e5 idle alike (18.3 and 18.2 us) and differ in the clock, which rises at 47.5 in the one and 37.8 in the other. But e16, e5's order all but two moves, rose at 49.5, so one profile of each does not show that the order did it. The last section has what may be a part of it.
